# Infini-attention beside a feed-forward block on one core: eight PSUM banks dealt 3/3/2 throughout, or dealt anew as 4/3/1 behind the projections

## The chip, the cores and the metric

One core of a Trainium2 chip runs the whole program. The metric is the device time of one execution in microseconds (us). The kernel before was timed three times: 564.6, 566.44 and 569.66, median 566.44.

## The reference, cut to what matters

Sequence 2048, width 448, 16 heads of 28, four segments of 512 tokens, hidden width 1792.

```python
q, k, v = x @ wq, x @ wk, x @ wv          # 16 heads, 4 segments of 512
for s in range(4):
    p = softmax(q_s k_s^T * scale + causal mask)
    o = g * (phi(q_s) M) / (phi(q_s) z) + (1 - g) * (p @ v_s)
    M, z = M + phi(k_s)^T v_s, z + sum(phi(k_s))
a = concat(o) @ wo
b = silu(x @ w1) @ w2
out = gate * a + (1 - gate) * b           # gate = sigmoid(sum(x * gate_w))
```

## The kernel before, in words

The program has three parts. `project()` computes the projections q, k and v, the memory matrix M and what is read from it, in fp32r matmuls. Then come sixteen attention groups (`attention(t)`, four heads each) together with the first pass of the feed-forward block (`ffn(0, ...)`, hidden blocks 0 to 9). At the end stand the second pass (blocks 10 to 13) and the products with `wo`.

After the projections every product is of fp16 pieces, a high and a low half, so that one feed-forward product of 512 columns (`unit`, line 617) is 11 matmuls. On its PSUM bank work four more instructions in turn: tanh on ACT (L1163), a multiplication in place on DVE (L1165), the high half on ACT (L1167), and the low half on DVE (L1169). Only then is the bank free. Ten such products make one segment's first half, and then four products with `w2` (L1186, 30 matmuls each) use banks of the same set.

For each group `maxima` finds the rows' maxima: score matmuls (L718, L722) into "sc" banks, read by DVE (L732, L727), and a transpose (L740). For each head, `attention` computes the scores again, transposed, into three "sc" tiles (L1284), which ACT turns into exponentials (L1289); POOL masks them (L1292, L1295), ACT makes the high half (L1301), POOL the low half (three L1305); then P times V is 20 small matmuls (L1318) into one "cc" bank, which DVE sums out (L1326).

The order of all this is not written by hand. `Sched` is a list scheduler in Python: each task has an engine, a modelled duration, dependencies, a priority `prio`, and the buffers that it takes. It plays the program through on its own clock, and each engine's instructions are issued in the order that comes out. A task that takes a PSUM bank can't start before the bank that was taken `n` takings earlier is free, where `n` is the bank count of its ring (`start_of`). `HOP` is the time that the planner allows from one engine's end to another engine's start: HA stands in ACT's, HD in DVE's. `PRICE` weighs uncovered weight loads on PE, `PVP` and `LOP` set when P times V and the low half of P are due, `FLO` and `FHI` spread the feed-forward's due times, `MAXO` sets the maxima's, and `WOT` and `WOP` set those of the products with `wo`. On the chip the waits are semaphores on data and buffers alone; the planner's clock only sets the order.

`BANKS` (line 37) deals the eight banks: three "mm" for projections and feed-forward products, three "sc" for scores, v and the products with `wo`, two "cc" for the memory, the retrieval and P times V. A `Ring` hands out its tiles in turn.

Of the kernel before, what the change touches and what calls it, by code (L numbers as in the profile page):

```python
# [8 lines left out]
F32 = mybir.dt.float32  # L9
# [7 lines left out]
PSUM = bass.MemoryType.PSUM  # L17
# [17 lines left out]
COLD = 5.0  # L35
WARM = 15
BANKS = {"mm": 3, "sc": 3, "cc": 2}
FREE = FB - 1
PASSES = [list(range(0, 10)), list(range(10, FB))]
CUTS = (384, 896)  # L40
# [1 line left out]
UP = 2.0 ** 14  # L42
DOWN = 2.0 ** -24
TINY = 2.0 ** -40
WOT = 67.47
TUS = 1.6
TLAT = 4.0

HP = 0.18
HA = 0.3  # L50
HD = 0.21
HO = 0.09
HS = 0.14
PQL = 0.5
AB = 1.92
PA0 = 0.53
SLACK = 0.88
LOP = 13.0
LATE = 0.08
FIRST = 120.0  # L60
WPRIO = 120.0
MAXO = 65.49
FULL = 0.111
LOCK = 0.06
RB = "cc"
# [15 lines left out]
    return o + VA + VS * k if o or k > VF else -1.0 + 0.1 * k  # L81


PRICE = 35.99
PVRUNS = [((1, 0), 1)]
PVP = 39.68
FLO = -13.66
FHI = 698.15
WOP = 108.16
SZ = 22.8  # L90
SZSTEP = 2.6
XPRIO = 72.99
# [24 lines left out]
class Sched:  # L117

    HOP = {"PE": 0.2 + HP, "ACT": 0.145 + HA, "DVE": 0.13 + HD, "POOL": 0.1 + HO, "SP": 0.1 + HS}
    SAME = {"PE": 0.0, "ACT": 0.0, "DVE": 0.1, "POOL": 0.1, "SP": 0.0}
# [59 lines left out]
    def matmuls(self, ready):  # L182
# [3 lines left out]
        def rank(t):  # L186
            nxt = leads[0] if t.lead != leads[0] or len(leads) == 1 else leads[1]
            if len(leads) == 1 or t.lead == leads[0] and leads[1] != leads[0]:
                nxt = FULL
            return t.prio[0] + PRICE * (max(0.0, t.lead - self.tail) + max(0.0, nxt - t.tail)), t.prio[1]  # L190
        return min(ready, key=rank)
# [54 lines left out]
def infini_mix(ctx: ExitStack, tc: tile.TileContext, x, wq, wk, wv, wo, beta, w1, w2, out):  # L246
# [16 lines left out]
    onescr = dram("one_scr", (2, 4, L), F16)  # L263

    const = ctx.enter_context(tc.tile_pool(name="const", bufs=1))
    psum = ctx.enter_context(tc.tile_pool(name="psum", bufs=1, space=PSUM))

    def raw(ap):
        return ap.bitcast(F32)
# [1 line left out]
    def tiles(pool, name, shape, dt, n, tag=None):  # L271
        return Ring(n, lambda: pool.tile(shape, dt, name=name, tag=tag or name, bufs=n), pool is not psum)
# [8 lines left out]

    BK = {n: tiles(psum, n, [128, 512], F32, k) for n, k in BANKS.items()}

# [23 lines left out]
    def pool(cols, fn, *deps, **k):  # L307
        return sch.add("POOL", 0.1 + 0.0019 * cols, fn, deps, **k)
# [29 lines left out]
    cols, at = {}, 0  # L338
    for j, n in [(j, 4) for j in range(NSEG)] + [(W1, FREE), (W2, FB), (WO, 4)]:
        cols[j] = (at, at + n)  # L340
# [310 lines left out]
    def get_wa(f, ring, prio, *deps, got=None):  # L651
        (r, d), w = got or fetch_wa(f, prio, *deps), Buf(ring)

        def v():
            return r.v.rearrange("p (a b) -> p a b", a=4)
        WA[f] = (w, halves(W1, (slice(None), slice(0, 4)), [((slice(None), slice(4, 8)), (slice(None),), (slice(None), slice(0, 4)))],
                           lambda: w.v, v, L, d, prio, takes=[w], uses=[r]))
        return WA[f][1]
# [39 lines left out]
    def maxima(t, o):  # L698
# [12 lines left out]
        for q, (i, hs) in enumerate(plan):  # L711
            ps = Buf(BK["sc"])
            n = 128 * (i + 1)
            p0 = o - MAXO + 40 * q / len(plan)

# [37 lines left out]
    def project():  # L753
# [328 lines left out]
        for t in range(NT):  # L1082
# [19 lines left out]
            if s < NSEG - 1:  # L1102
                memory(t, o + MP)
        pieces = [(W1, w1[f], L, total) for f in range(FREE)] + [(W2, w2[f], D, total) for f in range(FB)]
        for i, (j, src, n, how) in enumerate(pieces):
# [23 lines left out]

    FW = []  # L1130
    project()

    fes = ExitStack()
    fp = fes.enter_context(tc.tile_pool(name="ffn", bufs=1, reuse_waits="tile"))
# [16 lines left out]
    def unit(s, fs, prio, finish, gate=(), tail=False):  # L1151
        gt = {}
        t1, t2 = {}, {}
        for f in fs:
            if f == FREE:
                gt[f] = spare(s, prio(0), m)
# [51 lines left out]
    def spare(s, p0, m):  # L1208
        th, gf, g = Buf(TH), Buf(GF), Buf(GTR)
        if s not in SP:  # L1210
            fetch_spare(s, p0)
        h, e0 = SP[s]
        e1 = copy(L + 110, lambda: nc.scalar.activation(th.v, h.v, AF.Tanh, scale=wide[:, NSEG + s:NSEG + s + 1]), e0, m,
                  takes=[th], uses=[h], prio=p0)
        e2 = dve(L, lambda: nc.vector.scalar_tensor_tensor(gf.v, th.v, 1.0, h.v, op0=OP.add, op1=OP.mult), e1,
                 port=True, takes=[gf], uses=[h, th], prio=p0)
        e3 = copy(L + 110, lambda: nc.scalar.activation(g.v[:, 0], gf.v, AF.Copy, scale=hso[:, s:s + 1]), e2, m, takes=[g],
                  uses=[gf], prio=p0)
        e4 = scaled(L, lambda e: rest(e, g.v[:, 1], gf.v, hso[:, s:s + 1], g.v[:, 0]), e3, uses=[gf, g], prio=p0)
        return g, [e3, e4]  # L1220
# [8 lines left out]
    def weights(fs, t1, t2, prio):  # L1229
        for j, f in enumerate(fs):  # L1230
            if f != FREE:
                get_wa(f, WAR, prio, t1[max(j - 1, 0)])
# [29 lines left out]
    def attention(t):  # L1262
# [9 lines left out]
        for hh in range(4):  # L1272
# [31 lines left out]
            for u, w in zip((0,) + CUTS, CUTS + (1280,)):  # L1304
                low = pool(w - u, lambda hl=hl, flat=flat, u=u, w=w: nc.gpsimd.tensor_sub(  # L1305
                    hl.v[:, 1, u:w], flat()[:, u:w], hl.v[:, 0, u:w]), low, uses=[pf, hl], prio=p0 + LOP,
                    lat=0.0 if w < 1280 else LATE)
            ps = Buf(BK["cc"])
            last = None
            for zs, ready in PVRUNS:  # L1310
                def go(zs=zs, ps=ps, hl=hl, hh=hh):
                    p = ps.v[:, :TB * 58].rearrange("p (i t e) -> p i t e", i=TB, t=2)
                    off = (0, 512, 1024, 896)
                    for z in zs:
                        for i in range(TB):
# [5 lines left out]
                last = pe([m for z in zs for m in [(max(x, 0.027), y) for x, y in half((58, 29)[z], 10)]], go, dv, (hi, low)[ready], last,  # L1321
                          takes=[ps] if last is None else [], uses=[ps, hl, vg], prio=p0 + PVP)

            def fin(hh=hh, ps=ps):
                p = ps.v[:, :TB * 58].rearrange("p (i t e) -> p i e t", i=TB, t=2)
                nc.vector.tensor_reduce(orw.v[:, hh], p, axis=AX.X, op=OP.add)  # L1326
            fins.append(dve(232, fin, last, *fins[:1], takes=[] if fins else [orw], uses=[ps, orw], prio=p0 + PVP))
        rl, ob = Buf(C["rl"]), Buf(C["ob"])
# [12 lines left out]
    for i, f in enumerate(PASSES[0][NA:]):  # L1341
        get_wa(f, WAR2, FLO - 20 + i, got=FW[i] if i < len(FW) else None)
    for i, f in enumerate(PASSES[0]):
        get_wb(f, WBR, WBP + 2 * i, fetch_wb(f, WBP + 2 * i))
    for t in range(NT):
        attention(t)
    prio = spread(FLO, FHI, NSEG * len(PASSES[0]) * (11 * L + TB * 3 * D))
    ends = ffn(0, prio, part)
# [25 lines left out]
    wos, rw = Buf(later("wos", [128, 8, D], F16, 1)), Buf(later("rwo", [128, 4, D], F32, 1))  # L1374
    d = dma(1032e3, lambda: start(rw.v, wo), *attended, takes=[rw], prio=FHI)
    WOS = {}
    for c in range(NC + 1):
        ALL = slice(None)
        WOS[c] = halves(WO, (ALL, c), [((ALL, 4 + c), (ALL,), (ALL, c))], lambda: wos.v, lambda c=c: rw.v[:, c], D, d,
                        FHI + 10, takes=[] if c else [wos], uses=[rw, wos])  # L1380

    def last_part(s, tb, ps, lasts, prio):
        k = s * TB + tb
        ol, pl, oh, ot, pw, a, y = Buf(OL), Buf(PL), Buf(OH), Buf(OT), Buf(BK["sc"]), Buf(AR), Buf(YR)
        pr = prio - WOP
        rows = slice(tb * 128, (tb + 1) * 128)
        more = (Buf(ML), attended, amscr[s][:, tb]) if s else None
        d1 = load_o(ol, oscr[s][rows, :], *OST[s], PRE.get("o"), more=more, prio=pr - WOP)
        d2 = dma(229e3, lambda: start(pl.v, pscr[s][rows, :]), PST[k], *attended, PRE.get("p"),
                 takes=[pl], prio=pr - WOP)  # L1390
        PRE.update(o=d1, p=d2)
        ft = features(ol, oh, ot, [d1, outer, PRE.get("f")], pr - WOT)
        m = product(lambda: pw.v[:, :D], lambda: passes(wos.v, ot.v, True), D, pr,
# [10 lines left out]

    ffn(1, spread(FHI + 20, FHI + 1020, NSEG * len(PASSES[1]) * (11 * L + TB * 3 * D)), last_part)
    sch.run([outer] + attended)
# [26 lines left out]
def _layouts(A_x, A_wq, A_wk, A_wv, A_wo, A_beta, B_x, B_w1, B_w2, gate_w):  # L1433
# [8 lines left out]
        "x": xs,  # L1442
        "wq": _packed(_woven(A_wq, w1[:, FREE * 128:FREE * 128 + 64])),
        "wk": _packed(_woven(A_wk, w1[:, FREE * 128 + 64:])),
        "wv": _packed(vg),
# [28 lines left out]
```

## Time and profile before

| what | value |
|---|---|
| profiled execution's own time | 565.89 us |
| its span (first to last instruction) | 564.2 us, so 1.7 lie around it |
| median of three timed runs | 566.44 us |
| granted TensorE clock, mean | 0.992 |
| busy: PE / DVE / ACT / POOL | 545.9 / 409.3 / 405.7 / 392.5 us |
| first feed-forward matmul | 152.7 us |
| last P times V | 470.6 us |

PE's busy time counts a matmul until its modelled end, so that short waits between matmuls partly vanish in it; the distance from one start to the next shows them. Times in the views are counted from the span's start. A row of the timeline gives start, length, engine, line, operation, tiles, count, and in brackets the idle time before it and what ended that.

### The profile page before, as it was taken

Reading aid. Unit: us, or ns where it says so; the run is one execution under the profiler, and the core shown is the slowest. Engines: PE = TensorE matmul, PEld = TensorE weight load, DVE = VectorE, ACT = ScalarE, POOL = GpSimd, SP = SyncE. Lnnn points to the kernel's source line nnn. Section 1 sums busy time; section 2 is a strip of 40 time slices with the busy share of each in tenths; the row PEclk is TensorE's granted clock in tenths of the full one; section 3 lists DMA queues with packets and bytes.
Section 4 is the critical chain, followed back from the end, with each engine's and each line's share of the span. In section 5 each row is a group of like instructions: output and inputs, shape, how many; then the busy total and the mean of one; then the engine's idle time right before and its main releaser. Section 6 shows DMA issues by size and latency. Waiting matters only on the chain.

```text
span 564.2 us, 11666 instructions
## 1 busy us (share of the span) xinstructions
PE 545.9 (97%) x4015; PEld 336.4 (60%) x4015; DVE 409.3 (73%) x1043; ACT 405.7 (72%) x707; POOL 392.5 (70%) x603
## 2 busy tenths in 40 slices
PE   8999999999899999989999999999999999999997
PEld 4788878888544555555555555655555554554544
DVE  6885888888889967887755878876886219745563
ACT  7969789956567988989677988768997796303240
POOL 4938868786312889989879988999999993212210
PEclk9999999999999999999999999999999999999999
DMA  8797788957766444333324333436501125689841
GB/s 290 222 241 230 209 218 236 255 138 226 203 188 172 123 135 143 113 103 81 87 77 145 85 86 118 120 119 169 118 22 36 51 83 155 177 232 259 236 124 65
DMA packets 91499, 85.88 MB, mean 152 GB/s; under 512 B 55432, under 2 KB 79112, under 8 KB 91440
## 3 DMA queue, kind: packets, MB, share of 16 engines
q1 hardware_dynamic: 91440, 85.15, 53.4%
q8 instruction: 31, 0.51, 0.4%
q14 instruction: 28, 0.23, 0.1%
HBM read 52.60 MB, written 26.09 MB: 139 GB/s over the span
## 4 chain that ended last, share of the span: by engine, by line
PE 79%; DVE 11%; POOL 3%; issue 3%; DMA 2%; ACT 1%; SPq 0%; DVEq 0%; POOLq 0%
PE mm L617 30%; PE mm L1186 21%; PE sc L617 10%; PE sc L1284 5%; PE sc L722 5%; PE cc L1318 5%; DVE sc L732 3%; POOL phl L1305 1%; DVE xh L569 1%; DVE ghl L1169 1%; DMA raw<-in_wv_dram 1%; PE cc L1000 1%; DMA rawf<-in_x_dram 1%; DVE mm L1165 1%; PE cc L1043 1%
## 5 line engine op out<-in xcount | busy, mean ns | idle before, releaser
L1305 POOL TENSOR_TENSOR phl<-pf,phl 128x384 f16<-128x384 f32 (+1 forms) x192 | 193.4, 1028 | 14.3 <-ACT phl L1301 14.1
L1186 PE MATMUL mm<-wb,ghl 128*128 128x448 f16 (+1 forms) x684 | 147.2, 349 | 2.1 <-DVE ghl L1169 2.1
L617 PE MATMUL mm<-xh,wa 128*128 128x512 f16 x572 | 144.6, 384 | 1.2 <-DVE ghl L1169 1.0
L732 DVE CUSTOM_DVE_ANT_0 sc<-sc,mk 128x384 f32<-128x384 f32 (+1 forms) x192 | 105.5, 570 | 31.4 <-PE sc L722 29.7
L1289 ACT ACTIVATE pf<-sc,es 128x512 f32<-128x512 f32 (+1 forms) x192 | 109.9, 616 | 23.2 <-PE sc L1284 20.4
L1186 PEld LDWEIGHTS <-ghl 128*128 128x128 f16 x684 | 64.3, 97 | 56.1 <-issue 5.9
L617 PEld LDWEIGHTS <-wa 128*128 128x128 f16 x572 | 54.6, 98 | 57.6 <-issue 6.7
L1301 ACT ACTIVATE phl<-pf 128x1280 f16<-128x1280 f32 x64 | 81.1, 1269 | 8.1 <-POOL pf L1295 7.7
L1284 PE MATMUL sc<-ring 86*128 86x512 f16 (+3 forms) x256 | 59.6, 302 | 4.6 <-DVE mx L732 2.3
L722 PE MATMUL sc<-ring 84*128 84x128 f16 (+3 forms) x256 | 58.4, 299 | 0.9 <-ACT pf L1289 0.6
L1163 ACT ACTIVATE th<-mm,ths 128x512 f32<-128x512 f32 x52 | 35.3, 686 | 19.9 <-PE mm L617 19.6
L628 POOL TENSOR_TENSOR ol<-ol,ml 128x448 f32<-128x448 f32 x12 | 13.6, 1134 | 49.4 <-DMA ol<-o_scr 41.4
L1318 PEld LDWEIGHTS <-phl 128*128 128x128 f16 x1280 | 41.8, 96 | 8.6
L617 PE MATMUL mm<-xT,wqs 128*128 128x512 f32 x176 | 46.8, 404 | 0.0
L617 PE MATMUL mm<-xT,wks 128*128 128x512 f32 x176 | 46.6, 400 | 0.0
L1318 PE MATMUL cc<-vg,phl 128*128 128x29 f16 (+1 forms) x1280 | 43.8, 182 | 0.0
L1326 DVE TENSOR_REDUCE oraw<-cc 128x116 f32<-128x232 f32 x64 | 25.0, 392 | 22.0 <-PE cc L1318 21.9
L1165 DVE SCALAR_TENSOR_TENSOR mm<-th,mm 128x512 f32<-128x512 f32 x52 | 35.8, 692 | 7.3 <-ACT th L1163 7.1
L617 PE MATMUL sc<-wvs,xT 128*128 128x450 f32 x176 | 40.4, 374 | 0.0
L1284 PEld LDWEIGHTS <-ring 86*128 86x128 f16 x256 | 24.4, 98 | 26.2 <-issue 4.3
L1169 DVE SCALAR_TENSOR_TENSOR ghl<-mm,ghl 128x512 f16<-128x512 f32 x52 | 35.2, 681 | 5.0 <-ACT ghl L1167 4.8
L1167 ACT ACTIVATE ghl<-mm 128x512 f16<-128x512 f32 x52 | 30.7, 597 | 10.7 <-DVE mm L1165 10.7
(194 smaller groups left out, 917.7 us busy)
## 6 DMA issues: line engine op xcount, KB each, us to landing
rawf<-in_w_dram SPq DMA_DIRECT2D x26, 256.0 KB
rawf<-in_w_dram SPq DMA_DIRECT2D x28, 224.0 KB
xraw<-in_x_dram SPq DMA_DIRECT2D x16, 256.0 KB
rawf<-in_x_dram SPq DMA_DIRECT2D x16, 256.0 KB
v_scr<-vt SPq DMA_DIRECT2D x16, 232.0 KB
vg<-v_scr SPq DMA_DIRECT2D x16, 232.0 KB
q_scr<-stg SPq DMA_DIRECT2D x16, 224.0 KB
ring<-q_scr SPq DMA_DIRECT2D x16, 224.0 KB
```

The costliest lines, as they stand in the source:

```text
L617: nc.tensor.matmul(ps(), *p[i], start=(i == 0), stop=(i == n - 1))
L722: nc.tensor.matmul(ps.v[:, u:u + n], rg.v[:KS, 0, hh, i * 128:(i + 1) * 128], rg.v[:KS, 1, hh, :n], start=(i > 0), stop=(i > 0 or j == 3), ...
L732: nc.vector.tensor_tensor_reduce(r, r, MK[:, L - n:], 1.0, NEG, OP.add, OP.max, mx.v[:, hh, i:i + 1])
L1163: e1 = sact(L, lambda ps=ps, th=th: nc.scalar.activation(th.v, ps.v, AF.Tanh, scale=ths[:, s:s + 1]), m, takes=[th], uses=[ps], prio=p0)
L1165: e2 = dve(L, lambda ps=ps, th=th: nc.vector.scalar_tensor_tensor(ps.v, th.v, 1.0, ps.v, op0=OP.add, op1=OP.mult), e1, uses=[ps, th], prio=p0)
L1169: e4 = dve(L, lambda ps=ps, g=g: nc.vector.scalar_tensor_tensor(g.v[:, 1], ps.v, DOWN, g.v[:, 0], op0=OP.mult, op1=OP.subtract), e3, uses= ...
L1186: nc.tensor.matmul(ps.v[:, lo:hi], g.v[:, y, sl], w.v[:, z, lo:hi], start=(j == 0 and i == 0), stop=(j == len(fs) - 1 and i == 2))
L1284: nc.tensor.matmul(ps.v[:, e:e + w], rg.v[:KK, 1, hh, j * 128:(j + 1) * 128], rg.v[:KK, 0, hh, j * 128:], start=True, stop=True)
L1289: ex.append(sact(e, lambda b=b, ps=ps, pf=pf, e=e: nc.scalar.activation(pf.v[:, b, :e], ps.v[:, :e], AF.Exp, scale=es[:, s:s + 1]), m, *ex ...
L1301: hi = copy(1280, lambda hl=hl, flat=flat: nc.scalar.activation(hl.v[:, 0], flat(), AF.Copy), *mk, takes=[hl], uses=[pf], prio=p0 + 2)
L1305: low = pool(w - u, lambda hl=hl, flat=flat, u=u, w=w: nc.gpsimd.tensor_sub(hl.v[:, 1, u:w], flat()[:, u:w], hl.v[:, 0, u:w]), low, uses=[ ...
L1318: nc.tensor.matmul(p[:, i, :2 - z], hl.v[:, z, u:u + 128], vg.v[:, j, hh, :2 - z], start=(z == zs[0] and i == 0), stop=(z == zs[-1] and j ...
```

## The change

Behind `project()` the PSUM pool is closed and a second one is opened. Its tiles wait only for the earlier users of their own bank (`reuse_waits="tile"`). The rings are made anew from `BANKS2`: four banks for feed-forward products, three for scores, one for P times V. Ten numbers of the planner have other values. The operations and their shapes are the same; lines below the first edit stand one to five lower.

```diff
 BANKS = {"mm": 3, "sc": 3, "cc": 2}
+BANKS2 = {"mm": 4, "sc": 3, "cc": 1}
-WOT = 67.47
+WOT = 57.06
-HA = 0.3
-HD = 0.21
+HA = 0.16
+HD = 0.17
-LOP = 13.0
+LOP = 10.28
-MAXO = 65.49
+MAXO = 69.07
-PRICE = 35.99
+PRICE = 37.03
-PVP = 39.68
-FLO = -13.66
-FHI = 698.15
-WOP = 108.16
+PVP = 47.57
+FLO = -10.11
+FHI = 656.8
+WOP = 113.63
...
-    psum = ctx.enter_context(tc.tile_pool(name="psum", bufs=1, space=PSUM))
+    pes = ExitStack()
+    psum = pes.enter_context(tc.tile_pool(name="psum", bufs=1, space=PSUM))
...
     project()
+    pes.close()
+    psum = ctx.enter_context(tc.tile_pool(name="psum2", bufs=1, space=PSUM, reuse_waits="tile"))
+    BK.update((n, tiles(psum, n + "2", [128, 512], F32, k)) for n, k in BANKS2.items())
```

The planner writes the whole order anew. Three places on PE show it. The first is PE in the third ten feed-forward products (segment 2), before. The numbers in the names count tiles; with three "sc" banks a tile gets the bank of the third "sc" tile ahead of it. Weight loads and repeats are left out.

```order
L722 MATMUL sc_4803<-ring0_529 128x384
L1318 MATMUL cc_4809<-vg_4085,phl_4666 128x29
...
L722 MATMUL sc_4834<-ring0_529 128x512
L722 MATMUL sc_4838<-ring0_529 128x384
L722 MATMUL sc_4842<-ring0_529 128x512
L1284 MATMUL sc_4847<-ring0_529 128x512
L1284 MATMUL sc_4852<-ring0_529 128x384
L1284 MATMUL sc_4852<-ring0_529 128x128
L1318 MATMUL cc_4857<-vg_4085,phl_4748 128x29
...
L1284 MATMUL sc_4881<-ring0_529 128x256
L1284 MATMUL sc_4885<-ring0_529 128x512
L617 MATMUL mm_4888<-xh2_2226,wa_2178 128x512
```

The same engine and the same ten products in the changed kernel:

```order
L724 MATMUL sc2_4787<-ring0_652 128x384
L724 MATMUL sc2_4790<-ring0_652 128x512
L619 MATMUL mm2_4732<-xh2_2228,wa_2186 128x512
...
L724 MATMUL sc2_4799<-ring0_652 128x384
L619 MATMUL mm2_4801<-xh2_2228,wa2_2271 128x512
...
L1289 MATMUL sc2_4811<-ring3_2226 128x512
L619 MATMUL mm2_4801<-xh2_2228,wa2_2271 128x512
...
L1289 MATMUL sc2_4820<-ring3_2226 128x384
L1289 MATMUL sc2_4820<-ring3_2226 128x128
L1289 MATMUL sc2_4823<-ring3_2226 128x256
```

Before, seven "sc" tiles stand there with no feed-forward matmul among them, and two heads' P times V on the two "cc" banks; now feed-forward matmuls stand between the score tiles.

The second place is PE between two P times V groups that stand closest in the changed kernel (segment 3). Both go into the one "cc" bank.

```order
L1323 MATMUL cc2_5792<-vg_5027,phl_5681 128x58
L724 MATMUL sc2_5815<-ring0_652 128x512
L724 MATMUL sc2_5817<-ring0_652 128x384
L619 MATMUL mm2_5768<-xh3_2229,wa_1868 128x512
...
L724 MATMUL sc2_5828<-ring0_652 128x512
L619 MATMUL mm2_5768<-xh3_2229,wa_1868 128x512
...
L1289 MATMUL sc2_5833<-ring3_2226 128x512
L1323 MATMUL cc2_5836<-vg_5027,phl_5743 128x29
```

Between the two groups stand five feed-forward matmuls and four score tiles; before, each group has the bank of the last but one.

The third place is PE behind the last P times V, before and then in the changed kernel, up to the first product with `wo`.

```order
L1318 MATMUL cc_7283<-vg_6534,phl_7186 128x58
L617 MATMUL mm_7261<-xh1_2225,wa_6074 128x512
...
L617 MATMUL mm_7372<-xh2_2226,wa_6074 128x512
...
L1186 MATMUL mm_7440<-wb_7347,ghl_7334 128x448
L617 MATMUL sc_7464<-wos_7444,oT_5831 128x448
```

```order
L1323 MATMUL cc2_7333<-vg_6584,phl_7251 128x58
L619 MATMUL mm2_7317<-xh2_2228,wa_6041 128x512
...
L1191 MATMUL mm2_7462<-wb_7371,ghl_7354 128x448
L619 MATMUL mm2_7405<-xh2_2228,wa_6203 128x512
L619 MATMUL sc2_7492<-wos_7479,oT_5600 128x448
```

Before, 35 feed-forward matmuls of 512 columns and 36 of 448 stand between; now it is 24 and 36.

On the other engines seven low halves that POOL made (lines 571 and 572) go over to DVE (line 569, net), so that DVE has seven instructions more and POOL fourteen fewer.

## Prediction

> **What bounds the kernel now.** I read the page first, then busy time by stretch, cut at the first and last matmul of each segment's ten feed-forward products, then the waits of PE, then the places where PE lost time.
>
> ```profile
> PE 545.9 (97%) x4015; PEld 336.4 (60%) x4015; DVE 409.3 (73%) x1043; ACT 405.7 (72%) x707; POOL 392.5 (70%) x603
> ```
>
> ```profile
> core 0: us, PE busy (x) PEld busy (x) DVE busy (x) ACT busy (x) POOL busy (x), PEclk, DMA share, GB/s
> 152.70:183.40 30.70, 29.71 (x137) 13.32 (x135) 26.17 (x68) 19.26 (x32) 5.62 (x9) 0.94 0.65 187
> 183.40:222.10 38.70, 37.67 (x359) 22.51 (x358) 30.57 (x80) 33.71 (x54) 33.55 (x44) 1.00 0.44 130
> 222.10:262.10 40.00, 38.54 (x342) 21.16 (x341) 30.77 (x88) 35.77 (x58) 37.64 (x51) 1.00 0.34 98
> 262.10:305.00 42.90, 40.66 (x389) 23.98 (x388) 29.06 (x87) 30.79 (x50) 37.97 (x54) 1.00 0.37 102
> 305.00:349.10 44.10, 42.97 (x414) 24.03 (x413) 33.57 (x94) 40.32 (x64) 39.88 (x56) 0.96 0.33 98
> 349.10:388.00 38.90, 38.25 (x358) 22.52 (x357) 29.67 (x95) 29.16 (x47) 36.93 (x52) 1.00 0.48 134
> 388.00:425.40 37.40, 37.01 (x338) 20.62 (x337) 31.59 (x89) 35.44 (x59) 36.87 (x50) 1.00 0.37 91
> 425.40:461.00 35.60, 34.67 (x349) 20.61 (x348) 12.05 (x34) 28.70 (x44) 34.26 (x50) 1.00 0.17 54
> ```
>
> PE sets the time, at 97%, and its work is the same in both kernels. So the question is only how much time PE loses between matmuls. Busy time hides part of that, so I price the work. These are PE's groups in 152.7 to 461, and three pieces of the chain of waits that hold matmuls back to back:
>
> ```profile
> L617 PE MATMUL mm<-xh,wa 128*128 128x512 f16 x443 | 115.3, 385 | 1.2 <-DVE ghl L1169 1.0
> L1186 PE MATMUL mm<-wb,ghl 128*128 128x448 f16 x480 | 108.9, 352 | 2.1 <-DVE ghl L1169 2.1
> L1284 PE MATMUL sc<-ring 86*128 86x512 f16 (+3 forms) x256 | 59.6, 302 | 4.6 <-DVE mx L732 2.3 <-ACT pf L1289 1.3
> L722 PE MATMUL sc<-ring 84*128 84x384 f16 (+2 forms) x240 | 54.8, 299 | 0.9 <-ACT pf L1289 0.6 <-DVE mx L732 0.2
> L1318 PE MATMUL cc<-vg,phl 128*128 128x29 f16 x1220 | 41.8, 182 | 0.0
> L718 PE MATMUL sc<-maskb,identb 128*128 128x512 bf16 x15 | 5.7, 378 | 0.0
> ```
>
> ```profile
> 471.30 7.55 PE mm L617 x35
> 478.85 6.81 PE mm L1186 x36
> 485.66 8.32 PE sc L617 x44
> ```
>
> A matmul of 512 columns takes 7.55/35 = 0.2157 us, one of 448 takes 6.81/36 = 0.1892. The difference over 64 columns gives 0.00041 a column and 0.004 for each matmul, so four score matmuls of one head (1280 columns) take 0.545. Twenty small ones take 0.52 (a row further down: 0.68 less the last one's tail of 0.352 - 0.189 = 0.16). The work is 443 x 0.2157 = 95.6, 480 x 0.1892 = 90.8, 64 heads x 0.545 = 34.9, 60 x 0.545 = 32.7, 61 x 0.52 = 31.7, 15 x 0.2157 = 3.2, and about 1.8 for a score of single small ones: 290.7. The stretch is 308.3 long. PE loses 17.6 there.
>
> **Where they go.** First the clock.
>
> ```profile
> 320.70:323.60 2.90, 2.03 (x29) 0.95 (x25) 2.90 (x12) 2.21 (x4) 2.90 (x4) 1.00 0.58 164
> 323.60:327.00 3.40, 3.40 (x22) 1.66 (x18) 3.21 (x5) 2.31 (x4) 2.67 (x4) 0.50 0.00 0
> 263.20:265.80 2.60, 1.43 (x12) 0.50 (x9) 2.57 (x10) 2.60 (x5) 2.60 (x3) 1.00 0.42 107
> ```
>
> Half clock for 3.4 costs 1.7. The same stands once more at 152.7 (0.94 x 30.7 leaves 1.8 away). That is 3.5, and 14.1 remain. Four waits in it are single late results:
>
> ```profile
> 190.49 0.54 PE L1186 MATMUL mm<-wb,ghl 128*128 128x448 f16 x2 [1.03 <-DVE ghl L1169]
> 253.87 0.38 PE L1284 MATMUL sc<-ring 86*128 86x512 f16 x1 [0.42 <-ACT pf L1289]
> 273.96 0.27 PE L1284 MATMUL sc<-ring 86*128 86x256 f16 x1 [1.05 <-DVE mx L732]
> 433.70 0.27 PE L1284 MATMUL sc<-ring 86*128 86x256 f16 x1 [0.93 <-ACT pf L1289]
> ```
>
> With the tail of 0.16 that each hides, these are 4.1. The other 10 look like this, the first, one in the middle and the last of seven product starts of the kind:
>
> ```profile
> 176.62 0.68 DVE L1169 SCALAR_TENSOR_TENSOR ghl<-mm,ghl 128x512 f16<-128x512 f32 x1
> 177.35 1.46 PE L617 MATMUL mm<-xh,wa 128*128 128x512 f16 x6 [0.28 <-DVE ghl L1169]
> ```
>
> ```profile
> 240.53 0.59 PE L617 MATMUL mm<-xh,wa 128*128 128x512 f16 x2
> 250.20 0.68 DVE L1169 SCALAR_TENSOR_TENSOR ghl<-mm,ghl 128x512 f16<-128x512 f32 x1
> 250.93 0.59 PE L617 MATMUL mm<-xh,wa 128*128 128x512 f16 x2
> ```
>
> ```profile
> 409.54 0.77 PE L1284 MATMUL sc<-ring 86*128 86x384 f16 x3
> 409.85 0.69 DVE L1169 SCALAR_TENSOR_TENSOR ghl<-mm,ghl 128x512 f16<-128x512 f32 x1
> 410.58 0.81 PE L617 MATMUL mm<-xh,wa 128*128 128x512 f16 x3 [0.28 <-DVE ghl L1169]
> ```
>
> The low half that frees a bank ends at 177.30, 250.88, 410.54, and 0.04 to 0.05 later PE starts the product that takes this bank. The middle one is the product whose last matmul ended at 240.96: its bank was held for 9.9 us more, because the four instructions on it stand in the ACT and DVE queues among those of the attention. When all three "mm" banks are held so, PE has only scores left, and these run into their own three banks. The first order piece shows it: sc_4847 takes the bank of sc_4834, with 0.16 + 0.22 = 0.38 us of PE work between, but to read a tile of 512 columns DVE needs
>
> ```profile
> L732 DVE CUSTOM_DVE_ANT_0 sc<-sc,mk 128x512 f32<-128x512 f32 x57 | 40.3, 707 | 14.2 <-PE sc L722 14.1
> ```
>
> 0.71. That place is 320.7 to 323.6, where PE was busy 2.03 of 2.90, and 263.2 to 265.8 (1.43 of 2.60) is another. So a wait booked on "sc <- DVE mx" is often a lack of "mm" banks. Start to start, these places lose 9.3 of the 10.
>
> **The change part by part.** Fourth "mm" bank: I count PE work in both orders, at the unit prices, between a product's last matmul and the first into the same bank, for the ten-product runs of segments 1 to 3. Before it is 7.1 to 11.1 us, mostly about 8.2; now 10.9 to 12.9. The holds of these 30 products, read like the 9.9 above, were 4.6 to 11.1, so before they often exceed the distance, now nearly never. For "sc" tiles the distance is under 1.2 us in 21 of 371 cases before, in 1 of 372 now, the smallest 0.38 before and 1.03 now. The second order piece shows it. Worth: all 9.3 at best; nothing if the holds grow by as much. I take -9.3, since order and holds both say that the plan has no such gap left.
>
> Clock: the half-clock piece at 323.6 stands right behind one of these places, while 263.2 to 265.8 had none behind it. Between 0 and -1.7; neither row decides, so -0.9. The Trainium skill, "TensorE: Matmul & The Clock Gate", Part 1, says that the gate falls to half rate after an idle window of about 3.4 us and that the windows run freely. By that rule alone the sum would have the full -1.7 here, 0.8 less; the trace agrees with the length of the piece (3.40), but the window ahead of it was busy for 2.03 of 2.90, not idle.
>
> One bank for P times V: each group waits until DVE has summed out the one ahead. From the order the PE work between them is 1.9 to 6.7 us, middle 3.7 (before, over two banks, 4.2 to 12.1). The sum itself is short but can stand behind others:
>
> ```profile
> 357.11 0.68 PE L1318 MATMUL cc<-vg,phl 128*128 128x29 f16 x20
> 360.33 0.71 DVE L1326 TENSOR_REDUCE oraw<-cc 128x116 f32<-128x232 f32 x2
> ```
>
> This is the latest one: 2.7 us after its group's end (357.63), and with 0.4 for itself and 0.2 of hops the bank is free after 3.3. The middle one comes 0.6 late and frees after 1.2. Were all as the latest, 23 of 62 groups would wait, 12.4 in all; were they as the middle one, none. The planner now knows that the bank is single, so the middle row is nearer: +0.5, for a few late ones. The Trainium skill speaks against this edit: "Perfetto Trace Analysis", Optimizing Tensor Performance, Matmuls, has independent groups rotate through banks so that evacuation overlaps the next group. Taken alone it gives the 12.4; in this trace the next group stands 3.7 us of other work away.
>
> Behind the attention: 24 instead of 35 feed-forward matmuls of 512 columns stand between the last P times V and the first product with `wo`, so the distance falls from 14.36 (471.30 to 485.66) by 2.4 to 12.0.
>
> ```profile
> 480.92 2.33 ACT L577 ACTIVATE wos<-rwo,up 128x448 f16<-128x448 f32 x4
> 481.66 3.36 DVE L569 SCALAR_TENSOR_TENSOR wos<-rwo,up,wos 128x448 f16<-128x448 f32 x4
> ```
>
> The four low halves of `wo` are ready at 482.5 to 485.0. PE would want the first at 483.3 and the last, nine matmuls on, at 485.0: +0.3, between 0 and +1.
>
> Low halves from POOL to DVE: seven more on DVE.
>
> ```profile
> L569 DVE SCALAR_TENSOR_TENSOR xh<-rawf,up,xh 128x512 f16<-128x512 f32 x8 | 8.2, 1050 | 0.0
> ```
>
> At this length they are 7.4 over the whole run. They lie beside PE, since DVE is busy 71% of 183.4 to 461 (197 of 277.6). Without that cover, in the runs of ten products (31.59 of 37.4), they cost up to 2; I take 0, as POOL loses fourteen in turn. New hop values in the planner move the projections a little; PE's distances there are alike, so 0, with 1.5 either way. The new pool's first products find banks that the projections left; nothing is queued ahead of them but the retrieval's last reads, as before: 0.
>
> Sum, against the profiled execution: 565.9 - 9.3 - 0.9 + 0.5 + 0.3 = **556.5 us**. That execution is 0.5 under the median 566.44 of the runs shown, well inside their spread, so I forecast the same number for the median.
>
> **The rivals.** *POOL or ACT is the next limit.* In 388.0 to 425.4 POOL is busy 36.87 and ACT 35.44 of 37.4. If PE stops losing time, the exponentials and low halves of P come late instead. POOL has 257 busy us in 183.4 to 461; at the 95% of 349.1 to 388.0 they need 271 instead of 277.6, a gain of at most 6.6. With two thirds of it reached, 4.5, the time is 561.4. Against it: fourteen instructions leave POOL.
>
> *The bank was not the cause.* If the holds grow with the distance, because the planner delays the four instructions, PE loses the same elsewhere: about 565.5. Against it: the product starts 0.05 us behind the release.
>
> *One bank for P times V decides, slower.* If DVE sums out as late as at 360.33 throughout, the 12.4 come in full; a stopped P times V stops the scores queued behind it on PE and so ACT and POOL, which have no slack to catch up. With the gain halved by that, 565.9 + 12.4 - 5 = 573. It decides from the point where sums come more than about 2 us late as a rule. Against it: the middle one is 0.6.
>
> **How the numbers follow.** Forecast 0.70, POOL or ACT 0.14, no effect 0.07, slower by the single bank 0.09. About 1%, 5.7 us, can be told from no change here: faster means under 560.8, slower over 572.1. The forecast's own range, 552.5 to 561, is almost all faster, and of the second rival a third is: 0.72. Slower is most of the last: 0.07. The rest, 0.21, is the same. For 8 in 10 the range runs from 552 (all waits, the clock and the late results gone) to 564.5, into the two middle rivals.
>
> **What would show it.** Right: in the runs of ten products no wait of PE ended by L1169 on L617; waits booked on "sc <- DVE mx" almost gone; the stretch from first feed-forward matmul to last P times V near its work; at most one half-clock piece in it; P times V waiting on L1326 below 1 us in all. Wrong: PE waits on L1326 of several us, or POOL and ACT near 100% with PE waiting on L1289 and L1305.

## The result, and the profile after

The changed kernel takes 561.75 us, the median of nine runs (560.66 to 563.51), against 566.44 for the kernel before (nine runs, 564.6 to 569.66): ratio 0.9919, with a 95% interval of 0.9896 to 0.9942. It is faster by 4.7 us, where 9.9 were forecast. Its profiled execution took 563.01 with a span of 561.3, which is 1.3 above its median; that of before was 0.5 below. So the two traces differ by 2.9 in the span, and the rest of the 4.7 is run-to-run; the other eight runs of the changed kernel had a granted clock of 0.992 to 0.994, the profiled one 0.990.

The first lines of the page of the changed kernel, busy time by engine:

```profile
PE 543.6 (97%) x4015; PEld 336.0 (60%) x4015; DVE 414.5 (74%) x1050; ACT 403.3 (72%) x707; POOL 376.7 (67%) x589
```

As before PE is at 97%, and as before this says nothing of where it loses time. The waits of PE over the whole changed kernel do (total, times, longest):

```profile
PE cc L1046 <- DVE phq L571: 3.8, 2, 2.2
PE cc L1045 <- DVE amr L1051: 2.3, 2, 1.8
PE mm L619 <- DVE ph L938: 1.9, 1, 1.9
...
PE mm L619 <- DVE ghl L1174: 0.9, 1, 0.9
PE sc L724 <- DVE mx L734: 0.6, 2, 0.4
PE sc L720 <- ACT pf L1294: 0.5, 1, 0.5
...
PE sc L1289 <- DVE mx L734: 0.2, 1, 0.2
```

The three that lead the list belong to the last projections and the retrieval. The waits that the change was about (products on the low half of g, scores on the maxima) have shrunk to single ones, and the one of 0.9 on the low half stands behind the attention. Busy time by stretch, cut at the first feed-forward matmul of each segment, shows the same; here the changed kernel:

```profile
core 0: us, PE busy (x) PEld busy (x) DVE busy (x) ACT busy (x) POOL busy (x), PEclk, DMA share, GB/s
146.20:158.90 12.70, 5.28 (x29) 3.46 (x28) 11.88 (x22) 7.46 (x12) 2.69 (x7) 0.80 0.73 221
158.90:163.70 4.80, 4.80 (x14) 1.77 (x13) 2.32 (x9) 0.00 (x0) 2.57 (x4) 0.50 0.50 165
163.70:226.20 62.50, 62.20 (x463) 33.79 (x462) 53.62 (x140) 50.71 (x82) 35.12 (x46) 1.00 0.57 157
226.20:302.00 75.80, 75.37 (x714) 43.59 (x712) 55.06 (x160) 64.92 (x103) 67.72 (x95) 1.00 0.34 98
302.00:378.70 76.70, 76.13 (x715) 43.50 (x713) 60.78 (x179) 63.72 (x101) 69.95 (x97) 1.00 0.42 116
378.70:453.50 74.80, 74.31 (x706) 42.81 (x704) 52.06 (x143) 65.53 (x107) 68.53 (x96) 1.00 0.32 87
```

and the second row's counterpart in the kernel before, from the same point to its first feed-forward matmul:

```profile
146.20:152.70 6.50, 4.05 (x28) 2.90 (x27) 6.32 (x11) 4.25 (x7) 1.50 (x3) 1.00 0.73 206
```

From segment to segment PE now idles about half a microsecond. But ahead of them there is a stretch of 12.7 us, 6.2 longer than before, in which it works 5.28.

For the comparison of kernels PE's lost time is counted in one way for all: each matmul's distance to the next start, less the distance that the fastest tenth of its kind has over all kernels here. This is stricter than the count in the prediction (20.1 for the stretch behind the entry to the last P times V, where that has 17.6 up to 461). PE's work summed so is 520.7 us in each kernel, and about 1.0 lies ahead of the first matmul. Entry means the first feed-forward matmul; all numbers are us. The runs below the first two rows are those of the section on the experiments.

| kernel | entry at | lost to the entry | lost from there to the last P times V | lost behind | after the last matmul | span | median |
|---|---|---|---|---|---|---|---|
| before | 152.7 | 17.9 | 20.1 | 0.3 | 4.1 | 564.2 | 566.44 |
| changed | 158.9 | 24.1 | 9.5 | 1.4 | 4.5 | 561.3 | 561.75 |
| deal_only | 153.2 | 18.5 | 11.0 | 3.1 | 4.7 | 558.9 | 560.82 |
| consts_only | 159.7 | 24.9 | 17.6 | 0.3 | 3.9 | 568.5 | 571.44 |
| split | 152.6 | 17.8 | 13.7 | 0.3 | 4.1 | 557.7 | 559.13 |
| mm3 | 158.2 | 23.5 | 21.7 | 3.0 | 4.3 | 574.2 | 575.67 |
| mm3_cc2 | 159.4 | 24.6 | 20.1 | 0.3 | 3.9 | 570.6 | 571.10 |
| mm3_sc4 | 158.9 | 24.2 | 25.9 | 4.1 | 4.4 | 580.3 | 581.59 |
| mm4_sc2_cc2 | 157.7 | 22.9 | 76.0 | 5.0 | 4.7 | 630.2 | 634.09 |
| scale_first | 154.0 | 19.2 | 14.0 | 0.3 | 4.3 | 559.6 | 561.94 |
| split_x165 | 153.3 | 18.5 | 20.1 | 0.3 | 3.9 | 564.6 | 567.26 |
| split_x180 | 152.5 | 17.7 | 21.6 | 0.7 | 4.2 | 566.0 | 567.99 |
| after_x165 | 158.6 | 23.8 | 27.5 | 0.3 | 4.1 | 577.5 | 579.44 |
| split_nox | 153.3 | 18.6 | 7.9 | 1.9 | 4.8 | 554.7 | 556.71 |
| after_nox | 158.7 | 23.9 | 8.6 | 0.3 | 4.0 | 558.6 | 559.55 |

The first two rows are the result: 10.6 us less lost in the stretch that the prediction spoke of, 6.2 more ahead of it, 1.0 and 0.5 more behind: -2.9.

### The profile page after: what moved, and what is told of

Read it like the earlier page. It is cut to its first block, busy times and chain, and to the rows that moved or that the text cites. A ratio compares the mean times of both kernels' runs of the same rounds, so it can differ in the third digit from the quotient of the medians.

```text
span 561.3 us, 11661 instructions
## 1 busy us (share of the span) xinstructions
PE 543.6 (97%) x4015; PEld 336.0 (60%) x4015; DVE 414.5 (74%) x1050; ACT 403.3 (72%) x707; POOL 376.7 (67%) x589
## 4 chain that ended last, share of the span: by engine, by line
PE 82%; DVE 7%; DMA 3%; ACT 2%; POOL 2%; issue 2%; SPq 0%; DVEq 0%; POOLq 0%; ACTq 0%
PE mm L619 31%; PE mm L1191 21%; PE sc L619 10%; PE sc L1289 6%; PE sc L724 6%; PE cc L1323 5%; DMA rawf<-in_x_dram 2%; DVE sc L734 1%; DMA raw<-in_wv_dram 1%; PE cc L1002 1%; PE sc L720 1%; DVE mm L1170 1%; DVE xh L571 1%; ACT pf L1294 1%; DVE phq L571 1%
## 5 line engine op out<-in xcount | busy, mean ns | idle before, releaser
L1310 POOL TENSOR_TENSOR phl<-pf,phl 128x384 f16<-128x384 f32 (+1 forms) x192 | 192.4, 1019 | 18.1 <-ACT phl L1306 17.9
L724 PE MATMUL sc<-ring 84*128 84x128 f16 (+3 forms) x256 | 57.1, 299 | 0.6 <-DVE mx L734 0.6
L619 PE MATMUL mm<-xT,wks 128*128 128x512 f32 x176 | 45.1, 397 | 1.9 <-DVE ph L938 1.9
L630 POOL TENSOR_TENSOR ol<-ol,ml 128x448 f32<-128x448 f32 x12 | 13.7, 1140 | 48.2 <-DMA ol<-o_scr 43.0
L1331 DVE TENSOR_REDUCE oraw<-cc 128x116 f32<-128x232 f32 x64 | 25.1, 392 | 22.6 <-PE cc L1323 22.3
L636 ACT ACTIVATE oh<-ol,os 128x448 f16<-128x448 f32 x16 | 10.7, 670 | 41.4 <-POOL ol L630 41.4
L1289 PEld LDWEIGHTS <-ring 86*128 86x128 f16 x256 | 24.2, 97 | 22.9 <-issue 0.7
```

The costliest lines, as they stand in the source:

```text
L619: nc.tensor.matmul(ps(), *p[i], start=(i == 0), stop=(i == n - 1))
L724: nc.tensor.matmul(ps.v[:, u:u + n], rg.v[:KS, 0, hh, i * 128:(i + 1) * 128], rg.v[:KS, 1, hh, :n], start=(i > 0), stop=(i > 0 or j == 3), ...
L1289: nc.tensor.matmul(ps.v[:, e:e + w], rg.v[:KK, 1, hh, j * 128:(j + 1) * 128], rg.v[:KK, 0, hh, j * 128:], start=True, stop=True)
```

## What makes the entry late

The retrieval's matmuls wait for results of ACT and DVE, and these for something else. Three pieces of the changed kernel's timeline, SP's queue, ACT and PE, follow the chain back (start, length, engine, line, operation, count, idle time before it and what ended it):

```profile
132.20 0.31 SPq L324 DMA_DIRECT2D q_scr<-stg  x1
136.06 0.52 SPq L324 DMA_DIRECT2D am_scr<-am  x1
136.67 1.06 SPq L324 DMA_DIRECT2D rawf<-in_x_dram  x2
```

```profile
135.80 0.69 ACT L919 ACTIVATE stg<-mm,sqk 128x512 f16<-128x512 f32 x1
142.23 0.72 ACT L579 ACTIVATE xh<-rawf,up 128x512 f16<-128x512 f32 x1 [5.74 <-DMA rawf<-in_x_dram]
142.85 0.62 ACT L969 ACTIVATE vt<-sc,sv 128x448 f16<-128x448 f32 x1
```

```profile
148.50 2.79 PE L619 MATMUL mm<-xT,wks 128*128 128x512 f32 x11 [1.88 <-DVE ph L938]
...
152.98 0.22 PE L1046 MATMUL cc<-mhl,phq 112*128 112x116 f16 x1 [1.57 <-DVE phq L571]
...
155.44 0.35 PE L1045 MATMUL cc<-mhl,phq 112*128 112x232 f16 x1 [1.79 <-DVE amr L1051]
157.97 0.28 PE L1046 MATMUL cc<-mhl,phq 112*128 112x116 f16 x1 [2.18 <-DVE phq L571]
```

The x that the feed-forward of segment 0 needs is loaded a second time (`rawf<-in_x_dram`), in two pairs. In the kernel before, SP issues the pairs here:

```profile
126.35 0.85 SPq L322 DMA_DIRECT2D rawf<-in_x_dram  x2
...
135.86 1.40 SPq L322 DMA_DIRECT2D rawf<-in_x_dram  x2
```

In the changed kernel the first pair is issued at 136.67, 10.3 later. In the plan it comes behind the scale of the two feed-forward weights, which a small matmul on PE starts at 117.55 before and at 122.16 now, behind the last scale of x instead of ahead of it; before first, then the changed kernel:

```profile
117.55 0.27 PE L425 MATMUL cc<-ident,most 128*2 128x128 f32 x1
```

```profile
122.16 0.27 PE L427 MATMUL cc<-ident,most 128*2 128x128 f32 x1
```

And in SP's queue it now stands behind a store that waits for POOL until 136.06. ACT reaches the scaling of this x at 136.5 and stands there for 5.74 us, with the scalings of v, q and k queued behind it. The waits of PE from 146 us on, shown above, are for results that come behind this; how much of the 6.2 us hangs on it, the run scale_first shows below. The Trainium skill, "TensorE: Matmul & The Clock Gate", in the section on architectural detail, has ACT and DVE take their instructions strictly in order; the 5.74 us agree, since nothing behind the x was started.

## The experiments

**deal_only and consts_only** part the change in two: the new banks with the old planner constants, and the old banks in one pool with the new constants.

The first, against the changed kernel, has all ten constants back at their old values:

```diff
-HA = 0.16
-HD = 0.17
+HA = 0.3
+HD = 0.21
...
```

The second, against the kernel before, has them at the new ones:

```diff
-HA = 0.3
-HD = 0.21
+HA = 0.16
+HD = 0.17
...
```

> New deal of the banks and new PSUM pool, all ten planner constants of the kernel before; so the order up to the end of the projections is that of the kernel before (the first 694 PE rows are the same). Theory A (the lost gain is the order of the projections, which the new hop values and the earlier start of the first scores change): first feed-forward matmul at 152 to 154 as before, PE's loss behind it below the 20.1 us of before, at 10 to 15; time 557 to 562. Theory B (the new pool itself delays the entry into the feed-forward): first feed-forward matmul at 157 to 159, time 562 to 567.

> Old deal of 3, 3 and 2 banks in one pool, all ten new planner constants. Theory A: the projections run in the order of the changed kernel, first feed-forward matmul at 157 to 160, and PE's loss behind it stays near the 20 us of before: 570 to 574, slower than before. Theory B: first feed-forward matmul at 152 to 154, time near 566.

Measured: 560.82 (ratio to before 0.9897, 0.9863 to 0.9932) with the entry at 153.2, and 571.44 (1.0087, 1.0058 to 1.0116) with the entry at 159.7. The new pool does not delay the entry; the new constants do, and alone they make the kernel slower by 5 us. deal_only also prices the new deal by itself: it has as much half clock as before (two pieces of 3.41 us, at 153.3 and 221.6), and PE loses 9.1 less in the stretch. Behind the attention it loses 2.8 more, in one wait of a product for its bank:

```profile
475.24 4.91 PE L619 MATMUL mm<-xh,wa 128*128 128x512 f16 x22 [2.68 <-DVE ghl L1174]
```

Of the ten only the two hop values and the lead of the maxima (`MAXO`) reach the planning of the projections: with these three at the old values the order up to there is that of the kernel before.

**split** keeps all of the change but those three during the projections.

```diff
-    HOP = {"PE": 0.2 + HP, "ACT": 0.145 + HA, "DVE": 0.13 + HD, "POOL": 0.1 + HO, "SP": 0.1 + HS}
+    HOP = {"PE": 0.2 + HP, "ACT": 0.145 + 0.3, "DVE": 0.13 + 0.21, "POOL": 0.1 + HO, "SP": 0.1 + HS}
...
+    lead = [65.49]
...
-            p0 = o - MAXO + 40 * q / len(plan)
+            p0 = o - lead[0] + 40 * q / len(plan)
...
     project()
+    Sched.HOP.update(ACT=0.145 + HA, DVE=0.13 + HD)
+    lead[0] = MAXO
```

> The changed kernel, but the planner uses the old hop values of ACT and DVE and the old lead of the maxima until the projections are planned, and the new ones behind that. Theory A: first feed-forward matmul at 152 to 154, PE's loss from there to the last P times V 9 to 12 us: 555 to 558, faster than both kernels. Theory B: first feed-forward matmul at 157 to 159, time 561 to 563. Theory C (POOL and ACT are the next limit and eat half of the gain): the entry comes earlier but the loss behind it grows by as much: 560 to 562.

Measured: 559.13 (0.9854, 0.9823 to 0.9886), the fastest version with the whole computation. The entry is at 152.6, as theory A had it, but the time is above its 555 to 558: of the 6.3 us less that PE loses up to the entry, 4.2 come back behind it.

**mm3** takes the fourth product bank away and gives it to nobody; **mm3_cc2** and **mm3_sc4** give it to P times V and to the scores, and **mm4_sc2_cc2** keeps it, but takes it from the scores instead of from P times V.

```diff
-BANKS2 = {"mm": 4, "sc": 3, "cc": 1}
+BANKS2 = {"mm": 3, "sc": 3, "cc": 1}
```

That is mm3; the others have 3, 3, 2, then 3, 4, 1, then 4, 2, 2 in this line.

> The changed kernel with three banks for feed-forward products instead of four (the eighth bank lies idle; scores keep three, P times V one). My theory of the fourth bank: PE's loss between the first feed-forward matmul and the last P times V goes back from 9.5 to 18 to 22 us, with waits of PE that end with the low half of g and with the maxima in the runs of ten products: 570 to 574. Theory C (POOL and ACT are the limit behind it): little changes, 561 to 564.

> The changed kernel with the old deal of 3, 3 and 2 banks in its second pool: beside the run with 3, 3 and 1 this differs by the second bank for P times V alone. My term (a single bank costs about 0.5): 574 to 577, the same as that run within 2. The rival (the single bank costs up to 12.4): 563 to 571.

> The changed kernel with three banks for products, four for scores and one for P times V. My theory (a wait booked on the scores' banks is a lack of product banks): no better than with three banks for scores, 572 to 577. Theory D (scores lacked banks, and any eighth bank would have done): 561 to 565.

> The changed kernel with four banks for products, two for scores and two for P times V. It tells what the fourth bank is best taken from. If the single bank for P times V costs as little as I forecast, taking it from the scores is worse: three score tiles in 1.0 us of PE's work and 0.71 us for reading one leave no slack with two banks: 565 to 572. If the single bank is what ate the gain: 556 to 560.

Measured: 575.67 (1.015, 1.012 to 1.018), 571.10 (1.0091, 1.0057 to 1.0124), 581.59 (1.0272, 1.0239 to 1.0305) and 634.09 (1.1234, 1.1183 to 1.1286). The first is 1.7 above the 570 to 574 that I had, the third 4.6 above its 577. Without the fourth bank PE loses 21.7 us in the stretch instead of 9.5, 12.2 more: 9.0 of it in single waits of over 0.15 us, start to start, and 2.6 at half clock. The waits are those that the prediction named (PE's waits there, then one of the places, both of mm3):

```profile
PE mm L619 <- DVE ghl L1174: 2.4, 5, 0.8
PE sc L1289 <- DVE mx L734: 1.9, 6, 0.5
```

```profile
189.13 0.38 PE L1289 MATMUL sc<-ring 86*128 86x384 f16 x2 [0.54 <-DVE mx L734]
189.34 0.85 PE L1323 MATMUL cc<-vg,phl 128*128 128x29 f16 x20
190.04 0.33 PE L1289 MATMUL sc<-ring 86*128 86x256 f16 x1
190.44 0.68 DVE L1174 SCALAR_TENSOR_TENSOR ghl<-mm,ghl 128x512 f16<-128x512 f32 x1
191.17 2.72 PE L619 MATMUL mm<-xh,wa 128*128 128x512 f16 x6 [0.80 <-DVE ghl L1174]
```

The low half ends at 191.12 and 0.05 later PE starts the product in its bank; ahead of it PE had scores alone and waited for the maxima. A fourth score bank in its stead cures nothing (25.9 lost, 12.1 of them at half clock), so the waits booked on scores were a lack of product banks. With the bank taken from the scores instead, the time is 72 us above the changed kernel's; the waits are P times V on the low half of P, and scores on their two banks:

```profile
PE cc L1323 <- POOL phl L1310: 11.0, 13, 1.8
PE sc L1289 <- DVE mx L734: 5.9, 10, 1.5
```

I had 565 to 572 for it: slower was right, the size was not. Of its 76.0 lost, 59.7 lie in one piece from 461.8 to 550.6, all at half clock (shown in the last section). From 460 to 546 PE issues no feed-forward matmul, neither products (line 619, here) nor those with `w2` (line 1191, the same row), so that it has attention alone; busy time of PE and PEld on that line:

```profile
460.00:546.00 86.00, 0.00 (x0) 0.00 (x0) 0.51 0.10 29
```

PE is busy for 59.6 us of it, which at full clock would be about 30 (my estimate, by halving). So the 72 us are not the price of a score bank beside products; what that is, this run does not show. And mm3 against mm3_cc2 is a miss of mine: I expected no difference, and the second P times V bank is worth 3 to 5 us beside three product banks (4.6 by the medians, 3.3 by the ratios, 3.6 by the spans). P times V itself waits for its bank 0.2 us in mm3. The rest comes from the order that the planner makes of it: 1.6 more lost in the stretch, 2.7 more behind it, 1.1 less ahead.

A second pool by itself is worth nothing: mm3_cc2 has the banks and the constants of consts_only and differs from it by that pool alone, with ratios of 1.0091 and 1.0087.

**scale_first** goes for the cause of the late entry alone, with all new constants in place.

```diff
-        END1.append(scales(W1, W2 + 1, WPRIO - 10))
+        END1.append(scales(W1, W2 + 1, 70.0))
```

> The changed kernel with all its new constants, but the planner's priority of the scale of the two feed-forward weights is 70 instead of 110, so that this step is planned ahead of the last scale of x again, and with it the x loads for the feed-forward come some ten places earlier in SP's queue, as in the kernel before. Theory A1 (the late scale and the late x loads behind it hold ACT's and DVE's queues and so the end of the projections): first feed-forward matmul at 152 to 155, time 555 to 559. Theory A2 (the hop values spoil the projections in another way): first feed-forward matmul stays at 157 to 159.5, time 561 to 563.

Measured: 561.94 (0.9934, 0.9911 to 0.9958), no better than the changed kernel. The first x load, and the entry:

```profile
126.45 0.37 SPq L324 DMA_DIRECT2D rawf<-in_x_dram  x1
```

```profile
153.51 0.22 PE L1046 MATMUL cc<-mhl,phq 112*128 112x116 f16 x1 [1.39 <-DVE phq L571]
...
154.02 1.44 PE L619 MATMUL mm<-xh,wa 128*128 128x512 f16 x4
```

So the mechanism of A1 is right: with the scale planned earlier x comes at its old place, and PE loses 4.9 us less up to the entry. The time of A1 is wrong: 4.5 us come back between the entry and the last P times V, as in split. Both lose them in one place. It is here in split, by stretch, with the last matmuls of the gap on PE and the end of x on DVE:

```profile
216.20:223.80 7.60, 3.96 (x37) 1.99 (x35) 6.00 (x17) 6.54 (x11) 4.78 (x8) 0.89 0.55 168
223.80:229.20 5.40, 5.40 (x16) 2.00 (x14) 1.10 (x4) 2.68 (x5) 5.40 (x8) 0.52 0.28 64
```

```profile
215.27 1.68 SPq L325 DMA_DIRECT2D rawf<-in_x_dram  x2
...
221.73 1.89 DVE L572 SCALAR_TENSOR_TENSOR xh<-rawf,up,xh 128x512 f16<-128x512 f32 x2
...
223.81 2.76 PE L620 MATMUL mm<-xh,wa 128*128 128x512 f16 x6
```

Segment 0's products end at 216.4; those of segment 1 can start when its x is scaled, at 223.62. In between PE has only attention to do, and behind that it runs at half clock for about 5 us. From 216 to 229 us split loses 7.6 us, 4.8 of it up to 222.2 and 2.9 at half clock behind that, and scale_first 7.1; the changed kernel loses 0.5.

**split_x165, split_x180, after_x165** raise the priority of x for the later segments.

```diff
-XLEAD = 146.82
+XLEAD = 165.0
```

The first has this on top of split, the second 180.0 there, the third 165.0 on top of the changed kernel.

> The run named split with the lead of the x loads for the feed-forward of segments 1 to 3 raised from 146.82 to 165: the planner now takes those of segment 1 three or four loads of the second weights earlier. In split PE has no product left from 216.2 to 223.8, because the second half of segment 1's x is loaded at 215.3 and ready at 223.6, and PE runs at half clock for some 5 us behind that: 3.6 and 2.5 us. Theory W (segment 1's x is the wall behind the repaired entry): this gap closes, 553 to 556. Theory C (exponentials and maxima are the next limit anyway): PE waits for scores elsewhere, 558 to 560.

> As the run before, with the lead at 180: the x loads of segment 1 come seven loads of the second weights earlier, and these weights later. Theory W: the gap at 216 to 224 is gone too, and it may come back ahead of the second products, which then wait for their weights: 552 to 558. Theory C: 558 to 560.

> The changed kernel itself, with its late entry (first feed-forward matmul at 158.9), and the lead of 165. Theory W: with the late entry the first segment's products last until x is there, so an earlier x brings nothing: 560 to 563. Theory C: the same 560 to 563; if it came out under 559, x was late in the changed kernel too.

Measured: 567.26 (1.0022, 1.0001 to 1.0043), 567.99 (1.0044, 1.0016 to 1.0072), 579.44 (1.0216, 1.0169 to 1.0263): all far off, for both theories. x and the ten pieces of the second weights go through the same two staging buffers, and where x goes first the second weights come late: the last matmul of segment 0 with `w2` starts at 239.3, 241.6 and 254.6, against 216.2 in split and 225.6 in the changed kernel. This says that the staging is full there, but not what ends the gap in split. The last two runs leave the disputed load out.

**split_nox and after_nox** leave out the loads, scalings and low halves of x for segment 1; its products read segment 0's x, so that this segment's feed-forward output is another one.

```diff
         deps = [derive(s, SCALED[NSEG - 1 - s], prio), *deps]
+        if s == 1:
+            X16[1], XH[1] = X16[0], [*XH[0], *deps]
+            return
```

> The run named split, with the x loads, scalings and low halves for the feed-forward of segment 1 left out: segment 1's products read segment 0's x (the output of that segment's feed-forward is another one). The order up to there stays. Theory W (behind the repaired entry PE waits until segment 1's x has come through the two staging buffers): the product gap of 216.2 to 223.8 and the half-clock piece behind it are gone, 551 to 555. Theory C (maxima and exponentials are the limit there): PE waits for scores as before, 557 to 559.5.

> The changed kernel with the same left out. Theory W: with the late entry the first segment's products last until 225.6 and x is there at 226.2, so little is to be had: 559 to 562. If x costs the changed kernel too (through DVE's and ACT's queues), it comes out at 555 to 558 like the other.

Measured: 556.71 (0.9844, 0.9818 to 0.9869) and 559.55 (0.9899, 0.9878 to 0.9921). The same two stretches in split_nox:

```profile
216.20:223.80 7.60, 7.34 (x79) 4.30 (x77) 4.31 (x14) 6.09 (x9) 6.57 (x10) 1.00 0.39 114
223.80:229.20 5.40, 5.40 (x46) 2.89 (x45) 3.78 (x11) 4.73 (x9) 5.17 (x8) 1.00 0.23 73
```

The gap and the half clock are gone, and segment 1 starts at 218.2 instead of 223.8. In after_nox it starts at 226.5, as in the changed kernel at 226.2, since there segment 0's products last until then. So theory W is right on the place: behind a repaired entry PE waits for segment 1's x. On the time it is right for the late entry (559 to 562 expected) and too hopeful for split: 5.9 us less are lost in the stretch, but 0.8 more ahead of it, 1.6 behind and 0.7 after the last matmul, in an order that the planner makes anew, and the span is 3.0 shorter, where I had 4 to 8 for the time. By the medians the time falls by 2.4; by the ratios, each taken beside its own runs of before, by 0.6 with some 2 either way. So that the wait for x makes the gap is shown; what the time gains by closing it is not.

## Why the prediction was half right, point by point

- **Fourth "mm" bank, -9.3: right.** No product waits for the low half of g in the stretch, scores on maxima wait 0.8 in all, mm3 brings the waits back, 9.0 us of them, and deal_only, with the old constants and equal half clock, loses 9.1 less than before. The order and the holds read from the trace were enough to price it, and the rival in which the holds grow with the distance falls.
- **Clock, -0.9: right in size, partly by luck.** Before, two half-clock pieces there cost 1.7 each; now one, at 158.9 to 163.7, costs 2.5: -0.8. The piece at 323.6 is gone whole, which would be the full -1.7; that the piece at the entry grew instead was not in the term.
- **Single late results, kept at 4.1: right.** Eight of 0.2 to 0.65 remain, 3.1 in all, read like the others from start to start.
- **One bank for P times V, +0.5: right for what it priced, nothing is waited for on L1331 in the changed kernel.** The rival at 573 falls with it. What a single bank costs through the order that the planner then makes was not in the term; beside three product banks it is 3 to 5, and beside four it was not tried by itself. The 0.2 of hops in the price of the rival is more than the traces show: DVE starts 0.04 after the matmul that it waits for, PE 0.05 after DVE.
- Together the stretch lost 10.6 less, where I had 9.7; the pieces above make 11.1, so 0.5 went in small distances.
- **Low halves of `wo`, +0.3: wrong in kind.** PE doesn't wait for them. Behind the attention 1.0 is lost on a product's bank (0.9 of it the wait on the low half of g listed above).
- **Low halves moved to DVE, +0: within its bounds of 0 to 2.** No run moved them alone.
- **"New hop values in the planner move the projections a little; PE's distances there are alike, so 0, with 1.5 either way": this step failed.** It measured +6.2 (lost to the entry, 17.9 and 24.1). The prediction looked at PE's distances alone. What moved was the place of one scale, and with it the first x loads in SP's queue, by ten microseconds; ACT then stood in front of the first of them. With that scale planned early again (scale_first) 4.9 of the 6.2 are gone; with the three old values in the projections (split), all. All signs that the prediction set for being right stand in the changed kernel's trace, but they lie behind the entry and could not show this.
- **What the sum could not hold.** Its terms were added as if independent. They are not: with the entry where I had it (split), the stretch loses 4.2 us more than in the changed kernel, 7.6 of its 13.7 at 216 to 229, because segment 1's x does not come earlier when PE does. In the changed kernel the late entry covers that. The sum was -9.4; the spans give -2.9 for the changed kernel and -6.5 for split (559.13 by its median, not 556.5). So of the 6.5 that are missing (5.2 by the medians), mending the entry brings 3.6; the other 2.9 stay, and split's loss at 216 to 229 alone is more than that.
- **POOL or ACT as the next limit, 561.4: the time was close, the mechanism was not it.** POOL is busy 67.72 of 75.80 in segment 1 and 69.95 of 76.70 in segment 2, and PE idles about half a microsecond in each.

Still open is what makes segment 1's x later in split (scaled at 223.6) than before (218.6): its second load pair waits for low halves that stand behind maxima in DVE's queue until 214.5, but no run moved these alone.

## What to carry to other kernels

Where several users take turns on a small set of banks, compare how long each holds a bank with how much of the waiting engine's work stands between two takings: here the bank belonged with the longest hold, and waits booked on another set were the lack of it. When a change alters what a planner assumes, read what moved on every queue, the DMA issuer's first, also in the stages that the change is not about. And before a repaired delay is counted as a gain, look for what arrives at its own time behind it.

## What the hardware showed that I had not expected

The half clock does not follow from the waits alone. Ahead of their first feed-forward matmul before and split have nearly the same work and waits, but not the same clock behind; before first, then split, each with its stretches cut once more:

```profile
148.00:152.70 4.70, 2.25 (x20) 1.46 (x19) 4.52 (x9) 2.48 (x4) 1.50 (x3) 1.00 0.67 181
152.70:156.20 3.50, 3.50 (x12) 1.30 (x10) 1.67 (x7) 0.72 (x1) 1.50 (x3) 0.53 0.81 257
...
149.52:152.93 3.41, 1.00 (x9) 0.71 (x10) 3.29 (x6) 1.91 (x3) 0.43 (x2) 1.00 0.69 200
```

```profile
148.00:152.70 4.70, 2.21 (x20) 1.56 (x20) 4.51 (x9) 2.36 (x4) 1.50 (x3) 1.00 0.65 189
152.70:156.20 3.50, 3.50 (x18) 1.56 (x16) 1.67 (x7) 0.90 (x2) 1.53 (x4) 1.00 0.79 251
...
147.10:150.50 3.40, 2.19 (x15) 1.41 (x13) 3.21 (x7) 2.49 (x5) 1.16 (x2) 1.00 0.65 199
150.50:153.92 3.42, 2.14 (x15) 1.25 (x16) 2.32 (x5) 0.74 (x2) 1.28 (x3) 1.00 0.66 174
```

In each of the fifteen traces all changes of the granted clock, but for the one at the program's end, lie on one grid of 3.413 us, and its place differs from trace to trace: the two pieces of before last 3.41 each and start 50 such steps apart (152.94 and 323.61), that of split lasts 6.83, that of the changed kernel 10.24. Cut on its own grid, before has PE busy for 1.00 of the 3.41 us ahead of the half clock, while in split the same work falls into two windows with 2.19 and 2.14. A busy share at which the clock falls does not come out of it: over all traces the windows ahead of a fall had PE busy for 0.08 to 0.76 of their length, and others with 0.47 and more kept the full clock.

And in mm4_sc2_cc2 the clock stayed at half for most of 86 us in which PE was busy for 59.6 and waited no longer than 1.8 at a time (the first and the last of four stretches):

```profile
460.00:480.00 20.00, 14.23 (x114) 7.24 (x114) 12.16 (x36) 13.24 (x21) 17.40 (x25) 0.55 0.16 48
...
520.00:546.00 26.00, 13.72 (x145) 7.93 (x143) 2.96 (x9) 15.41 (x21) 25.58 (x36) 0.50 0.07 19
```

The Trainium skill, "TensorE: Matmul & The Clock Gate", says in Part 1 that the windows run freely, with which the grids agree; its section on a second failure mode, psum-queue depth-cycling, has frequent short gaps between groups of matmuls make the clock oscillate. The second case has such gaps, but the clock did not oscillate: it stayed at half for 88.75 us and came back at 550.6, 3.9 us after PE's unbroken work began at 546.7.
